# Delta-rule attention and a low-rank mixer on one core: k, q and z of every second head moved to the other half of the partitions

## The chip, the core and the metric

One core of one Trainium2 chip (trn2) runs the whole program in one launch. The metric is the device time of that core in microseconds (us). TensorE (PE, with its weight loads PEld) multiplies matrices, VectorE (DVE), ScalarE (ACT) and GpSimd (POOL) work on tiles in on-chip memory, and SyncE (SP) issues most of the loads and stores (DMA). A tile has 128 partitions; here nearly everything is cut in two halves of 64 partitions, `half(0)` and `half(1)`. Results of matmuls land in PSUM, from where ACT or DVE copies them.

## What is computed

The input has 4 batches, 8 heads, 768 tokens and a head width of 48. For each head a state matrix is updated token by token, and its output is the query times the state before the update:

```python
k_n = k / (np.linalg.norm(k, axis=-1, keepdims=True) + 1e-06)
for t in range(S):
    kt, vt, bt = (k_n[:, :, t], v[:, :, t], beta[:, :, t, None])
    y[:, :, t] = np.einsum('bhd,bhde->bhe', q[:, :, t], state)
    v_old = np.einsum('bhde,bhd->bhe', state, kt)
    state = state + bt[:, :, :, None] * np.einsum('bhd,bhe->bhde', kt, vt - v_old)
```

The heads' outputs are put side by side as x (4 x 768 x 384). The mixer follows, with rank 32 over the tokens and a hidden width of 1536 over the channels:

```python
xt = x.transpose(0, 2, 1)
h = xt @ U @ V
u = x + h.transpose(0, 2, 1)
ch = np.maximum(u @ w_ch1, 0.0) @ w_ch2
return (u + ch).astype(np.float32)
```

All is fp32.

## The kernel before

The kernel works on the recurrence in chunks of 64 tokens (`L`), 12 per batch (`NC`). Half a batch, six chunks (`UC`), is a unit; units 0 and 1 are batch 0, units 2 to 7 are batches 1 to 3. Within a chunk, the tokens' mutual effect is a triangular matrix that is inverted (blocks of 32, `BK`), so that a chunk needs a few matmuls only.

Eight heads are laid out as two groups `g` of four slots `s = 2*j + par`. Group g has its tokens on partitions `half(g)`. After a transpose, the head's channels are on `half(par)`. `QUADS` lists the four (par, g):

```python
QUADS = ((0, 0), (1, 1), (1, 0), (0, 1))
heads = [(j, par, g) for j in range(2) for par, g in QUADS]
def half(i, size=L):
    return slice(L * i, L * i + size)
```

The rows that a matmul reads and the partitions that it writes decide which part of the 128 x 128 array it uses: reading `half(a)` and writing `half(b)` uses one 64 x 64 quarter.

The load puts all four slots of a group on its half:

```python
for s in range(4):
    engines[queue].dma_start(
        out=t[L * g : L * g + L, :, s],
        in_=src[b, 4 * g + s, hf * UC * L : (hf + 1) * UC * L, :].rearrange("(c t) d -> t c d", t=L),
    )
```

The Gram products of keys with keys and queries, in `grams`, two chunks a group (L501):

```python
for par, g in QUADS:
    rows, cols = slice(DP * par, DP * par + D), slice(L * g, L * g + L)
    nc.tensor.matmul(p_g[cols, par, c, parts, j], kq[rows, c0 + c, j, 0, cols],
                     kq[rows, c0 + c, j, parts, cols], start=True, stop=True)
```

For units 2 to 7 `parts` covers keys and queries at once, so the moving operand is 128 wide; units 0 and 1 do them apart, 64 wide.

The blocks below the diagonal of the inverse, for units 2 to 7 (`split == 1`), are two chains of 32 x 32 matmuls, 24 (`CS`) for each g. p_x (L673) reads the partitions from L*g + 32 and writes from 32*g; p_v (L690) reads from 32*g and writes from L*g:

```python
for i in range(4):
    nc.sync.dma_start(out=diagonal(zt, i), in_=blk[i])
for g in range(2):
    nc.sync.dma_start(out=zc[BK * g : BK * g + BK], in_=blk[2 * g])
turned(zn, zc)
...
p_x = ps_pair("p_x")
nc.tensor.matmul(p_x[BK * g : BK * g + BK, x, at], pg[rows, c, r, j, 0:BK], zt[rows, c, r, j, BK:L], ...)
nc.scalar.copy(xz, p_x[0 : 2 * BK, :, 0 : CS // 2 * BK])
p_v = ps_pair("p_v")
nc.tensor.matmul(p_v[L * g : L * g + BK, x, at], zn[BK * g : BK * g + BK, e], xz[BK * g : BK * g + BK, x, at], ...)
```

One step of the recurrence, in `recur` (cut): `from_state` (L849) reads the old state, z is the inverse times the right-hand side (p_c, L886, batches 1 to 3 only), p_s (L901) is the state's update and L909 adds z's part to the output:

```python
def from_state(p, kq, cu, i, s_old, first):
    for j, par, g in heads:
        nc.tensor.matmul(p[half(g), par, ...], kq[half(par, D), cu, j, i, half(g)], s_old[half(par, D), g, j], ...)
...
p_c = ps_one([128, 4, D], "p_c")
for j, par, g in heads:
    nc.tensor.matmul(p_c[half(g), 2 * j + par], zt[half(g), cu, par, j], rhs[half(g), 2 * j + par], ...)
nc.scalar.copy(z, p_c)
...
p_s = ps_pair("p_s")
for j, par, g in heads:
    nc.tensor.matmul(p_s[half(par), g, D * j : D * j + D], kn[half(g), cu, 2 * j + par], z[half(g), 2 * j + par], ...)
for j, par, g in heads:
    nc.tensor.matmul(p_y[half(g), par, D * (2 + j) : D * (2 + j) + D], qk[half(g), cu, par, j], z[half(g), 2 * j + par], ...)
```

PSUM comes in three pools of two buffers each: "pair" (two banks, `ps_pair`), "one" and "mix" (one bank each).

The order of all instructions is made while the program is built: each part of the work is a generator that yields steps with estimated durations per engine (`step(pe=..., act=..., take=("pair",))`), and a loop places the step that could start first. In the early phase it also fills TensorE's idle time with matmuls of no use (`keep_busy`, L106). The channel mixing of one batch (p_f at L1006, p_o at L1026, six records a group) runs between the attention steps of the next.

Of the kernel before, what the change touches and what calls it, by code (L numbers as in the profile page):

```python
# [16 lines left out]
L = 64  # L17
BK = 32
# [7 lines left out]
def kernel(  # L26
# [9 lines left out]
    moe_w_ch2: bass.AP,  # L36
    out: bass.AP,
):

# [104 lines left out]
    def run():  # L146
# [61 lines left out]
        out=upper, in_=upper, pattern=[[1, 128]], base=0,  # L208
        channel_multiplier=-1, compare_op=ALU.is_gt, fill=0.0,
    )  # L210
    mask_u = const.tile([128, L], FP32, name="mask_u")
    for g in range(2):
        at = slice(L * g, L * g + L)
# [36 lines left out]
    def load_beta():  # L250
        yield step(then=3.5)
        yield step(pe=1.2, then=0.1, take=("one",))
        p_bt = ps_one([128, NB, B, H], "p_bt")
        for c in range(NB):
            nc.tensor.matmul(
                p_bt[:, c].rearrange("p b h -> p (b h)"),
                beta_sb[:, c * 128 : c * 128 + 128],
                ident[0 : B * H, 0 : B * H],
                start=True,
                stop=True,  # L260
            )
        yield step(dve=0.8, give=("one",))
        for g in range(2):
            for i in range(2):
                nc.vector.tensor_copy(
                    out=betas[L * g : L * g + L, i::2].rearrange("p c (b s) -> p c b s", b=B),
                    in_=p_bt[L * i : L * i + L, :, :, 4 * g : 4 * g + 4],
                )
        emitted(("betas", 0))
# [97 lines left out]
    def load(n):  # L367
# [7 lines left out]
        vn = raw[n] = unit.tile([128, UC, 4, D], FP32, name="vn")  # L375

        def tensor(name, t, src, queues):
            if queues[0] != queues[1]:
                yield step(**{names[x]: 2.6 for x in queues})
            for g in range(2):  # L380
                queue = queues[g]
                if queues[0] == queues[1]:
                    yield step(**{names[queue]: 2.6})
                for s in range(4):
                    engines[queue].dma_start(  # L385
                        out=t[L * g : L * g + L, :, s],
                        in_=src[b, 4 * g + s, hf * UC * L : (hf + 1) * UC * L, :].rearrange(
                            "(c t) d -> t c d", t=L
                        ),
                    )  # L390
            emitted((name, n), 4.1 if n == 0 else 5.0)
# [19 lines left out]
    def norms(n):  # L411
# [15 lines left out]
        norm = small.tile([128, UC, 4], FP32, name="norm")  # L427
        nc.vector.tensor_reduce(out=norm, in_=ksq, axis=AX.X, op=ALU.add)
        emitted(("ksq", n))
        yield step(act=0.25, then=0.1)  # L430
        nc.scalar.sqrt(norm, norm)
        yield need(("betas", 0))
        yield step(dve=0.95, then=0.1)
        nc.vector.tensor_scalar_add(norm, norm, 1e-6)
# [36 lines left out]
    def grams(n):  # L471
# [22 lines left out]
        def products(c0, parts):  # L494
            yield step(pe=0.8 if parts.stop - parts.start == 1 else 1.4, then=0.1, take=("pair",))
            p_g = ps_pair("p_g").rearrange("p r (c i j t) -> p r c i j t", c=2, i=2, j=2)
            for c in range(2):
                for j in range(2):
                    for par, g in QUADS:
                        rows, cols = slice(DP * par, DP * par + D), slice(L * g, L * g + L)  # L500
                        nc.tensor.matmul(  # L501
                            p_g[cols, par, c, parts, j],
                            kq[rows, c0 + c, j, 0, cols],
                            kq[rows, c0 + c, j, parts, cols],
                            start=True,
                            stop=True,
                        )
            keys, queries = parts.start == 0, parts.stop == 2
            yield step(
                act=0.6 if keys and n > 0 else 0,  # L510
# [53 lines left out]
    def blocks(n):  # L564
# [86 lines left out]

        blk = [scr2[CS * i : CS * i + CS].rearrange("q s t -> s q t") for i in range(4)]
        if split == 1:
            yield step(sp=3.6, then=2.2)
            zc = single.tile([2 * BK, CS, BK], FP32, name="zc", tag="zc")
            zn = single.tile([2 * BK, CS, BK], FP32, name="zn", tag="zn")
            for i in range(4):
                nc.sync.dma_start(out=diagonal(zt, i), in_=blk[i])
            for g in range(2):
                nc.sync.dma_start(out=zc[BK * g : BK * g + BK], in_=blk[2 * g])  # L660

            yield step(dve=1.0, then=-0.8)
            turned(zn, zc)
            for e in range(CS):
                if e % 8 == 0:
                    yield step(pe=0.57, take=("pair",) if e == 0 else ())
                if e == 0:
                    p_x = ps_pair("p_x")
                c, r, j = e // 4, e // 2 % 2, e % 2
                x, at = e // (CS // 2), slice(BK * (e % (CS // 2)), BK * (e % (CS // 2)) + BK)  # L670
                for g in range(2):
                    rows = slice(L * g + BK, L * g + L)
                    nc.tensor.matmul(  # L673
                        p_x[BK * g : BK * g + BK, x, at],
                        pg[rows, c, r, j, 0:BK],
                        zt[rows, c, r, j, BK:L],
                        start=True,
                        stop=True,
                    )
            yield step(act=0.8, then=0.1, give=("pair",))  # L680
            xz = single.tile([2 * BK, 2, CS // 2 * BK], FP32, name="xz", tag="zc")
            nc.scalar.copy(xz, p_x[0 : 2 * BK, :, 0 : CS // 2 * BK])
            for e in range(CS):
                if e % 8 == 0:
                    yield step(pe=0.57, take=("pair",) if e == 0 else ())
                if e == 0:
                    p_v = ps_pair("p_v")
                x, at = e // (CS // 2), slice(BK * (e % (CS // 2)), BK * (e % (CS // 2)) + BK)
                for g in range(2):
                    nc.tensor.matmul(  # L690
                        p_v[L * g : L * g + BK, x, at],
                        zn[BK * g : BK * g + BK, e],
                        xz[BK * g : BK * g + BK, x, at],
                        start=True,
                        stop=True,
                    )
            yield step(act=1.6, give=("pair",))
            for g in range(2):
                rows = slice(L * g, L * g + BK)
                nc.scalar.mul(  # L700
                    zt[rows].rearrange("p (x c) r j t -> p x (c r j) t", x=2)[:, :, :, BK:L],
                    p_v[rows, :, 0 : CS // 2 * BK].rearrange("p x (q t) -> p x q t", t=BK),
                    -1.0,
                )
            for third in range(3):
                emitted(("below", n, third), 0.2)
            return
# [137 lines left out]
    def recur(b):  # L845
        def from_state(p, kq, cu, i, s_old, first):

            for j, par, g in heads:
                nc.tensor.matmul(  # L849
                    p[half(g), par, D * (2 * i + j) : D * (2 * i + j) + D],  # L850
                    kq[half(par, D), cu, j, i, half(g)],
                    s_old[half(par, D), g, j],
                    start=first and j == 0,
                    stop=(i == 0),
                    skip_group_check=True,
                )
# [4 lines left out]
        for c in range(NC):  # L861
# [12 lines left out]
            if c > 0:  # L874
                for i in (0, 1) if b > 0 else (1, 0):
# [3 lines left out]
                nc.vector.tensor_tensor(  # L879
                    out=by_slot(rhs), in0=by_slot(raw[n][:, cu]), in1=pair_of(p_y), op=ALU.subtract  # L880
                )
            if b > 0:
                yield step(pe=0.4, then=0.1, take=("one",))
                p_c = ps_one([128, 4, D], "p_c")
                for j, par, g in heads:
                    nc.tensor.matmul(  # L886
                        p_c[half(g), 2 * j + par],
                        zt[half(g), cu, par, j],
                        rhs[half(g), 2 * j + par],
                        start=True,  # L890
                        stop=True,
                    )
                z = steps.tile([128, 4, D], FP32, name="z")
                yield step(act=0.33, then=0.1, give=("one",))
                nc.scalar.copy(z, p_c)  # L895

            yield step(pe=0.65, then=-0.2, take=("pair",) if c < NC - 1 else ())
            if c < NC - 1:
                p_s = ps_pair("p_s")
                for j, par, g in heads:  # L900
                    nc.tensor.matmul(  # L901
                        p_s[half(par), g, D * j : D * j + D],
                        kn[half(g), cu, 2 * j + par],
                        z[half(g), 2 * j + par],
                        start=True,
                        stop=True,
                    )
            for j, par, g in heads:
                nc.tensor.matmul(  # L909
                    p_y[half(g), par, D * (2 + j) : D * (2 + j) + D],  # L910
                    qk[half(g), cu, par, j],
                    z[half(g), 2 * j + par],
                    start=(c == 0 and j == 0),
                    stop=(j == 1),
                    skip_group_check=True,
                )
            yield step(
                dve=0.37 if c < NC - 1 else 0, act=0.65, on="dve", then=0.1,
                give=("pair", "pair") if c < NC - 1 else ("pair",),
            )  # L920
            if c < NC - 1:
                s_new = steps.tile([128, 2, 2, D], FP32, name="s")
# [168 lines left out]
```

## Time and profile before

| what | value |
|---|---|
| time, median of 3 runs | 717.27 us (716.61 to 717.34) |
| span in the profile | 715.6 us |
| PE busy | 669.1 us (93%) |
| PEld busy | 426.4 us (60%) |
| DVE busy | 325.6 us (45%) |
| ACT busy | 203.4 us (28%) |
| POOL busy | 42.5 us (6%) |
| p_f and p_o, PE busy | 201.0 and 201.2 us |

Busy time of PE counts the stretches in which at least one matmul is under way. Matmuls overlap, so a group's busy time is less than its count times the mean of one. A fp32 matmul shows as two records. In the lines of groups, `64*64 64x48` stands for the 64 rows and 64 columns of the array that the weights take, and for the moving operand, here 64 partitions by 48 elements; the number behind `x` is the count of records. Window and timeline views give times from the start of the span.

### The profile page before, as it was taken

The numbers are of one execution on the slowest core, as the hardware profiler recorded it, in microseconds if no ns is written. First come the engines' busy times: TensorE is split into PE (matmuls) and PEld (weight loads), VectorE is DVE, ScalarE is ACT, GpSimd is POOL, SyncE is SP. The second block draws the span as 40 slices with busy tenths as digits, with TensorE's granted clock in tenths as the row PEclk, the third lists the DMA queues.
The fourth block names the chain that finished last, engine by engine and source line by source line (L and its number), as shares of the span: only waits on it lengthen the run. The fifth ranks groups of instructions, "written<-read, shape, count | busy, mean of one in ns | idle before, by whom it ended". The sixth has DMA issues, their size and how long they took to land.

```text
span 715.6 us, 18968 instructions
## 1 busy us (share of the span) xinstructions
PE 669.1 (93%) x8370; PEld 426.4 (60%) x8370; DVE 325.6 (45%) x800; ACT 203.4 (28%) x468; POOL 42.5 (6%) x79
## 2 busy tenths in 40 slices
PE   6549999889999999889999999999999999899997
PEld 5336776646656566756566666556666665455554
DVE  7655777781775811459484113287483011200000
ACT  3314445454203211533122332243112311220110
POOL 4740010100000000000000000000000000000000
PEclk9768999999999999999999999999999999999999
DMA  8971558333124033351502050431402000000000
GB/s 142 210 155 33 128 122 203 104 67 74 40 55 79 4 66 64 66 115 31 111 13 63 12 97 25 92 66 30 84 23 57 3 12 24 1 0 23 11 1 33
DMA packets 140498, 45.37 MB, mean 63 GB/s; under 512 B 133568, under 2 KB 136640, under 8 KB 140416
## 3 DMA queue, kind: packets, MB, share of 16 engines
q1 hardware_dynamic: 130560, 30.39, 21.1%
q0 software_dynamic: 3552, 12.88, 6.4%
q10 hardware_dynamic: 6304, 0.89, 0.9%
q8 instruction: 66, 1.08, 0.7%
q14 instruction: 16, 0.13, 0.1%
HBM read 33.03 MB, written 11.11 MB: 62 GB/s over the span
## 4 chain that ended last, share of the span: by engine, by line
PE 82%; DVE 8%; DMA 4%; ACT 2%; SPq 2%; issue 1%; ACTq 0%; DVEq 0%
PE p_f L1006 27%; PE p_o L1026 24%; PE p_y L849 3%; PE p_c L886 3%; PE p_y L909 3%; PE p_g L501 3%; PE p_h L965 2%; PE p_s L901 2%; PE p_t L486 2%; DVE prod L621 2%; DVE xt L627 2%; SPq L385 2%; PE p_x L673 1%; PE p_v L690 1%; DVE x L969 1%
## 5 line engine op out<-in xcount | busy, mean ns | idle before, releaser
L1006 PE MATMUL p_f<-ut,w_sb 128*128 128x384 f32 x576 | 201.0, 494 | 1.1 <-ACT ut L976 1.1
L1026 PE MATMUL p_o<-w_sb,h_f 128*128 128x384 f32 x576 | 201.2, 495 | 0.6 <-DVE x L996 0.6
L1026 PEld LDWEIGHTS p_o<-w_sb,h_f 128*128 128x128 f32 x576 | 104.7, 190 | 65.2 <-DVE x L996 1.2
L1006 PEld LDWEIGHTS p_f<-ut,w_sb 128*128 128x128 f32 x576 | 104.4, 190 | 64.4 <-ACT ut L976 1.6
L991 ACT ACTIVATE h_f<-p_f 128x384 f32<-128x384 f32 x96 | 47.2, 491 | 185.9 <-PE p_f L1006 185.9
L996 DVE TENSOR_TENSOR x<-x,p_o 128x384 f32<-128x384 f32 x24 | 13.2, 553 | 134.8 <-PE p_o L1026 134.8
L627 DVE TENSOR_TENSOR xt<-xt,prod 96x112 f32<-96x112 f32 (+21 forms) x216 | 70.4, 326 | 7.4
L621 DVE TENSOR_TENSOR prod<-gs,xt 96x112 f32<-96x112 f32 (+21 forms) x216 | 70.0, 324 | 8.0 <-ACT xt L597 1.5
L924 DVE TENSOR_TENSOR s<-s,p_s 128x192 f32<-128x192 f32 x40 | 14.1, 354 | 77.1 <-PE p_s L901 77.0
L931 ACT COPY x<-p_y 64x192 f32<-64x192 f32 x96 | 30.1, 313 | 67.0 <-PE p_y L909 57.9
L879 DVE TENSOR_TENSOR rhs<-vn,p_y 128x192 f32<-128x192 f32 x44 | 15.5, 353 | 54.9 <-PE p_y L849 54.3
L492 ACT COPY kq<-p_t 128x512 f32<-128x512 f32 x48 | 27.9, 585 | 33.9 <-PE p_t L486 26.7
L849 PEld LDWEIGHTS p_y<-s,kq 48*64 48x64 f32 x1408 | 25.0, 134 | 18.8 <-issue 16.3
L895 ACT COPY z<-p_c 128x192 f32<-128x192 f32 x36 | 11.5, 320 | 70.2 <-PE p_c L886 69.5
L849 PE MATMUL p_y<-s,kq 48*64 48x48 f32 x1408 | 30.4, 222 | 0.2
L501 PEld LDWEIGHTS p_g<-kq 48*64 48x64 f32 x960 | 22.7, 137 | 12.8 <-issue 7.4
L501 PE MATMUL p_g<-kq 48*64 48x128 f32 (+1 forms) x960 | 28.6, 258 | 1.3 <-ACT kq L492 1.2
L577 POOL MEMSET xt<- 96x1056 f32 x6 | 5.9, 978 | 351.3 <-DMA scr<-xt 351.3
L886 PEld LDWEIGHTS p_c<-rhs,zt 64*64 64x64 f32 x528 | 18.6, 134 | 13.5 <-issue 7.9
L523 DVE TENSOR_TENSOR qk<-p_g,mask_u 128x256 f32<-128x256 f32 x48 | 18.0, 416 | 19.0 <-ACT pg L517 18.4
L886 PE MATMUL p_c<-rhs,zt 64*64 64x48 f32 x528 | 22.4, 222 | 2.1 <-DVE rhs L879 1.2
L909 PE MATMUL p_y<-z,qk 64*64 64x48 f32 x576 | 22.9, 218 | 0.9 <-ACT z L895 0.9
(149 smaller groups left out, 637.5 us busy)
## 6 DMA issues: line engine op xcount, KB each, us to landing
wide<-in_moe_w_ch_dram POOLq DMA_DIRECT2D x6, 768.0 KB, 5.4
stage<-in_moe_w_ch_dram POOLq DMA_DIRECT2D x6, 768.0 KB, 5.3
out_dram<-x SPq DMA_DIRECT2D x24, 192.0 KB, 1.9
kn<-in_k_dram SPq DMA_DIRECT2D x60, 72.0 KB, 4.0
qn<-in_q_dram SPq DMA_DIRECT2D x48, 72.0 KB, 2.4
vn<-in_v_dram SPq DMA_DIRECT2D x48, 72.0 KB, 2.4
gs<-scr SPq DMA_DIRECT2D x8, 384.0 KB, 3.7
scr<-xt SPq DMA_DIRECT2D x8, 384.0 KB, 3.0
```

Source lines behind the costliest of these rows:

```text
L492: nc.scalar.copy(places, p_t)
L501: nc.tensor.matmul(p_g[cols, par, c, parts, j], kq[rows, c0 + c, j, 0, cols], kq[rows, c0 + c, j, parts, cols], start=True, stop=True,)
L523: nc.vector.tensor_tensor(out=qk[:, at, par], in0=p_g[:, par, :, 1], in1=mask_u[:, None, None, :].to_broadcast([128, 2, 2, L]), op=ALU.mult,)
L621: nc.vector.tensor_tensor(out=prod, in0=gb[:, :, j : j + 1, j + 1 :].to_broadcast([NP, split, m, w]), in1=xb[:, :, 0:m, j : j + 1].to_broa ...
L627: nc.vector.tensor_tensor(out=xb[:, :, 0:m, j + 1 :], in0=xb[:, :, 0:m, j + 1 :], in1=prod, op=ALU.subtract,)
L849: nc.tensor.matmul(p[half(g), par, D * (2 * i + j) : D * (2 * i + j) + D], kq[half(par, D), cu, j, i, half(g)], s_old[half(par, D), g, j], ...
L886: nc.tensor.matmul(p_c[half(g), 2 * j + par], zt[half(g), cu, par, j], rhs[half(g), 2 * j + par], start=True, stop=True,)
L909: nc.tensor.matmul(p_y[half(g), par, D * (2 + j) : D * (2 + j) + D], qk[half(g), cu, par, j], z[half(g), 2 * j + par], start=(c == 0 and j ...
L931: nc.scalar.copy(tokens_of(b, c, g), pair_of(p_y, 1)[half(g)])
L991: nc.scalar.activation(hs[f], p_f, ACTF.Relu)
L1006: nc.tensor.matmul(p_f, w1_sb[:, t, f * 128 : (f + 1) * 128], ut[:, t], start=(t == 0), stop=(t == KT - 1),)
L1026: nc.tensor.matmul(p_os[c], hs[e][:, c * 128 : c * 128 + 128], w2_sb[:, e], start=(e == 0), stop=(e == FT - 1),)
```

## The change

Slots with odd `par` of k and q, and the right-hand side and z that go with them, are put on the other half of the partitions, so that the matmuls that read and write the same half use all four quarters of the array. v follows only in batch 0, where it is loaded crossed; in later batches p_c itself carries the odd heads across. The index `x` is now the half, not the head group. Where both are still mixed up, the kernel compensates: beta is transposed with a permuted identity (`swap`), the norms of odd heads are swapped by two small matmuls (`p_n2`), and the Gram products of odd heads write keys and queries to different halves, which needs two matmuls for each. p_c moves from a tile of its own to the spare part of the p_s tile. The blocks below the diagonal are spread over four tiles in each of the two chains. The diff, cut to its core (the rest renames g to x):

```diff
+    swap = const.tile([B * H, B * H], FP32, name="swap")
+    nc.gpsimd.tensor_copy(out=swap, in_=ident[0 : B * H, 0 : B * H])
+    for i in (0, 4):
+        nc.gpsimd.tensor_copy(
+            out=swap[:, i + 1 : i + 4 : 2], in_=ident[0 : B * H, 5 - i : 8 - i : 2]
+        )
...
-                ident[0 : B * H, 0 : B * H],
+                swap,
...
+            crossed = b == 0 or name != "v"
...
-                        out=t[L * g : L * g + L, :, s],
+                        out=t[half(g ^ (s % 2) if crossed else g), :, s],
...
-        yield step(act=0.25, then=0.1)
-        nc.scalar.sqrt(norm, norm)
+        if b == 0:
+            yield step(act=0.25, then=0.1)
+            nc.scalar.sqrt(norm, norm)
+        else:
+            yield step(pe=0.3, then=0.1, take=("one",))
+            p_n2 = ps_one([128, UC, 2], "p_n2")
+            for g in range(2):
+                nc.tensor.matmul(
+                    p_n2[half(g)], ident[:, half(1 - g)], norm[:, :, 1::2], start=True, stop=True
+                )
+            yield step(act=0.5, then=0.1, give=("one",))
+            nc.scalar.sqrt(norm[:, :, 0::2], norm[:, :, 0::2])
+            nc.scalar.sqrt(norm[:, :, 1::2], p_n2)
...
-                        nc.tensor.matmul(
-                            p_g[cols, par, c, parts, j],
+                        crossed = n > 1 and par == 1
+                        for i in (slice(0, 1), slice(1, 2)) if crossed else (parts,):
+                            to = half(1 - x) if crossed and i.start == 0 else cols
+                            nc.tensor.matmul(
+                                p_g[to, par, c, i, j],
...
-            zc = single.tile([2 * BK, CS, BK], FP32, name="zc", tag="zc")
+            HQ = CS // 2
+            zc = single.tile([128, HQ, BK], FP32, name="zc", tag="zc")
...
-            for g in range(2):
-                nc.sync.dma_start(out=zc[BK * g : BK * g + BK], in_=blk[2 * g])
+            for i in range(4):
+                x, g = divmod(i, 2)
+                nc.sync.dma_start(
+                    out=zc[BK * i : BK * i + BK], in_=blk[2 * g][:, HQ * x : HQ * x + HQ]
+                )
...
+            where = [(e, x, g) for e in range(HQ) for x in range(2) for g in range(2)]
+            yield step(pe=0.95, then=0.1, take=("one",))
+            p_x = ps_one([128, HQ, BK], "p_x")
+            for e, x, g in where:
+                q, rows, to = HQ * x + e, slice(L * g + BK, L * g + L), BK * (2 * x + g)
+                c, r, j = q // 4, q // 2 % 2, q % 2
+                nc.tensor.matmul(p_x[to : to + BK, e], pg[rows, c, r, j, 0:BK], zt[rows, c, r, j, BK:L], ...)
...
+            for e, x, g in where:
+                rows = slice(BK * (2 * x + g), BK * (2 * x + g) + BK)
+                nc.tensor.matmul(p_v[L * g : L * g + BK, x, BK * e : BK * e + BK], zn[rows, e], xz[rows, e], ...)
...
-                    p[half(g), par, D * (2 * i + j) : D * (2 * i + j) + D],
+                to = half(x if b == 0 and i == 0 else x ^ par)
+                    p[to, par, D * (2 * i + j) : D * (2 * i + j) + D],
...
-                yield step(pe=0.4, then=0.1, take=("one",))
-                p_c = ps_one([128, 4, D], "p_c")
+                yield step(pe=0.4, then=0.1, take=("pair",))
+                p_s = ps_pair("p_s")
-                        p_c[half(g), 2 * j + par],
-                        zt[half(g), cu, par, j],
-                        rhs[half(g), 2 * j + par],
+                        p_s[half(x), par, D * (2 + j) : D * (2 + j) + D],
+                        zt[half(x ^ par), cu, par, j],
+                        rhs[half(x ^ par), 2 * j + par],
-                nc.scalar.copy(z, p_c)
+                nc.scalar.copy(by_slot(z), pair_of(p_s, 1))
...
-                    p_y[half(g), par, D * (2 + j) : D * (2 + j) + D],
-                    qk[half(g), cu, par, j],
-                    z[half(g), 2 * j + par],
+                    p_y[half(x ^ par), par, D * (2 + j) : D * (2 + j) + D],
+                    qk[half(x), cu, par, j],
+                    z[half(x), 2 * j + par],
```

## The prediction, made blind

> **What bounds the kernel now.** I read the page first: the slices tell when TensorE is full, the chain of waits tells whose time it is.
>
> ```profile
> PE   6549999889999999889999999999999999899997
> PE 82%; DVE 8%; DMA 4%; ACT 2%; SPq 2%; issue 1%; ACTq 0%; DVEq 0%
> ```
>
> TensorE (PE) is 90% busy or more in most slices after the third, and 82% of the chain that ends last is its own work. A busy engine is not yet the bound, so I cut the span into stages (columns: window, busy time and count of each engine, PE clock, DMA share, GB/s):
>
> ```profile
> 150.00:606.00 456.00, 446.29 (x5554) 280.40 (x5554) 213.25 (x559) 128.61 (x287) 4.87 (x5) 1.00 0.24 51
> 606.00:623.00 17.00, 14.23 (x80) 7.61 (x76) 3.89 (x7) 4.18 (x10) 0.00 (x0) 1.00 0.00 1
> 623.00:716.00 93.00, 88.95 (x276) 52.06 (x274) 3.33 (x6) 11.32 (x24) 0.00 (x0) 1.00 0.04 13
> ```
>
> From 150 to 606 us the attention of batches 1 to 3 runs between the channel-mixing matmuls of the batch before. PE is busy 446 of 456 us (98%) at full clock, while VectorE (DVE) is at 213 of 456 (47%). A PE microsecond saved there should come off the span. From 623 us on only channel mixing is left, which the change does not touch. Before 150 us the kernel is a chain of loads, block inversion and weight conversion, with filler matmuls on PE.
>
> Now the cost of the matmuls that the change touches (columns: line, engine, form, count | busy us, mean ns of one | idle before):
>
> ```profile
> L909 PE MATMUL p_y<-z,qk 64*64 64x48 f32 x576 | 22.9, 218 | 0.9 <-ACT z L895 0.9
> L886 PE MATMUL p_c<-rhs,zt 64*64 64x48 f32 x528 | 22.4, 222 | 2.1 <-DVE rhs L879 1.2 <-issue 0.9
> L501 PE MATMUL p_g<-kq 48*64 48x128 f32 x576 | 19.8, 275 | 0.6 <-ACT kq L492 0.6
> ...
> L901 PE MATMUL p_s<-z,kn 64*64 64x48 f32 x528 | 14.8, 227 | 1.0 <-DVE qk L523 0.6 <-ACT z L895 0.5
> ...
> L673 PE MATMUL p_x<-zt,pg 32*32 32x32 f32 x576 | 10.6, 192 | 0.0
> L690 PE MATMUL p_v<-xz,zn 32*32 32x32 f32 x576 | 10.6, 192 | 0.0
> ...
> L501 PE MATMUL p_g<-kq 48*64 48x64 f32 x384 | 8.9, 234 | 0.7 <-ACT kq L492 0.6
> ```
>
> An fp32 matmul leaves two records: 36 steps (c of batches 1 to 3) x 8 matmuls are 288, and p_c has 528 + 48 = 576. The telling pair is p_c and p_s: same shape, same number, 22.4 us against 14.8. In the timeline (start, duration, what, count):
>
> ```profile
> 237.13 0.67 PE L886 MATMUL p_c<-rhs,zt 64*64 64x48 f32 x16
> 237.72 2.20 PE L1006 MATMUL p_f<-ut,w_sb 128*128 128x384 f32 x6
> 239.86 0.45 PE L901 MATMUL p_s<-z,kn 64*64 64x48 f32 x16
> 240.12 0.63 PE L909 MATMUL p_y<-z,qk 64*64 64x48 f32 x16
> 240.69 0.59 PE L1006 MATMUL p_f<-ut,w_sb 128*128 128x384 f32 x1
> ```
>
> From its first start to the next group's, p_s takes 0.26 us, p_y 0.57, p_c 0.59. Taking the last one's duration off the group (0.67 - 0.22, 0.45 - 0.23, 0.63 - 0.22) and dividing by 15 intervals, records start 30, 15 and 27 ns apart. The code says why: p_s reads rows of half g and writes half par, so its four (par, g) pairs are four quarters of the array; p_c and p_y at L909 read half g and write half g, so they use two of the four. Per quarter that is one record in about 60 ns in all three.
>
> **What the Trainium skill says.** "TensorEngine Tiling (Array Packing)", section "Tiling Modes", says that tiles work independently and can load weights and multiply in parallel, with four of them at 64x64. The trace agrees: twice the quarters, half the interval. The same page, "Gotcha 1: PSUM Pressure", says that different row tiles cannot access one PSUM bank at the same time. Here p_c writes a single bank from both row halves, to different partition halves, and its pace per quarter is that of p_s, which gives each row half a bank of its own; so no such cost is seen, and I expect none from the new placing, where both row halves share a bank on disjoint partitions. "TensorE: Matmul & The Clock Gate", section "Back-to-back issue gap", lists an issue floor of about 25 ns for small matmuls; p_s records start 15 ns apart over four quarters, so the measurement decides, and what the floor is for eight or more a wave no run here shows yet.
>
> **The change part by part.**
>
> *z on four quarters (p_c).* Odd heads of k, q (and z) now lie on the other half, so p_c reads half x^par and writes half x. 16 records at 15 instead of 30 ns: 0.225 us less per step (0.448 - 0.223). 36 steps: **-8.1 us**.
>
> *Output product on four quarters (p_y, L909).* Reads half x, writes half x^par: the same 0.2 to 0.24 us, 36 steps: **-8.1 us**. Batch 0 has 12 such groups as well, but before 150 us; see below.
>
> *Blocks below the diagonal (p_x, p_v).* Each uses two 32x32 tiles now and four after (eight different ones over both). 96 records a group at (1.77 - 0.19) / 95 = 16.6 ns, where 1.77 = 10.6 / 6 units. Half of that is 48 x 16.6 = 0.8 us a group, 12 groups: **-9.5 us** if four tiles really run at 8 ns a record. That is a faster stream of starts than anything in this trace sustains (the best is 15), so I count three quarters: **-7 us**.
>
> *Gram products (p_g).* For units 2 to 7 the odd heads' keys and queries now go to different halves, so each of their 128-wide products becomes two 64-wide ones: 32 records a group become 16 of 128 and 32 of 64. A quarter takes 4 x (1.10 - 0.275) / 31 = 106 ns for a 128-wide record, and 4 x (0.74 - 0.234) / 31 = 65 ns for a 64-wide one (1.10 = 19.8 / 18 groups, 0.74 = 8.9 / 12). The lower two quarters then have 16 x 65 = 1.04 us where they had 8 x 106 = 0.85: 0.19 us more, 18 groups: **+3.4 us**.
>
> *Norms.* Units 2 to 7 get two small matmuls (p_n2) that swap the halves of the odd heads' norms, and a second square root. A visit of PE costs its start as well as its records; from the p_ct rows and the 0.1 us that each group's first records take longer, I take 0.25 us a visit, 6 visits: **+1.5 us**. The extra ACT operation (about 0.22 us, the duration of the square root at L431) is on an engine at 28%.
>
> *Off the path.* The DVE transpose zn goes from 64x768 (967 ns) to 128x384, some 0.56 us by the 426 ns of its 128x256 form; the ACT copy xz from 792 to about 0.48 us. zc is loaded by four DMAs in place of two, same bytes. DVE and ACT have room, so I count nothing.
>
> *The start.* Three POOL copies build the swapped identity before the p_bt matmuls, which sit on the first stretch: POOL copies there take 0.24 us each, so up to +0.7 us. Batch 0's twelve output products save 12 x 0.22 = 2.7 us of PE; from 60 to 126 us the chain is on PE with its fillers, but from 127 to 158 us it is on DVE converting weights, which will take most of that back. Together **-0.5 us**.
>
> Sum: -8.1 - 8.1 - 7 + 3.4 + 1.5 - 0.5 = -18.8 us. The schedule is made at build time from estimated durations and now shifts; PE idles 2% in the stage already, and a shorter visit may meet a DVE or ACT result a little sooner than it is ready. A tenth off, -17 to -19: I take 717.3 - 18.3 = **699.0 us**.
>
> **The rivals.**
>
> *The recurrence's latency takes over.* Per step p_y, rhs (DVE 0.35), p_c, z (ACT 0.32), p_s, s (DVE 0.35) form a chain. Bare it is about 3 us, and one step takes 8.4 us in the trace (p_c at 228.69 and 237.13), because a 2.13 us group of p_f stands in every gap. There is slack, so I give this one chance in ten; the time would be about 708.
>
> *A new wait for PSUM.* p_c now lives in the two-buffer "pair" pool, in the tile that p_s uses later. So from p_c to the state update both pairs are taken, and the p_g and p_v groups have to find their place elsewhere. For it: 2.7 us of each step's 8.4. Against it: PE can run p_f meanwhile. If the groups pile up at a batch's end, as PE's idle from 606 to 623 us suggests is possible, it gives back 3 to 8 us: 703 to 708.
>
> *Small tiles bound by issue, not by the array.* If 16 records of 32x32 cannot start faster than now, p_x and p_v give nothing: 699 + 7 = 706.
>
> *Everything pays in full.* p_x and p_v at half, p_g nearly free because the quarters overlap: 693.
>
> **Range and chances.** The 2% line is 702.9 us. The first two parts (16 us) rest on a measured pair of rows and alone reach 701, but the added p_g and p_n2 work takes 5 back; p_x and p_v decide on which side it falls. Range 691 to 707; faster 0.72, within 2% 0.26, slower 0.02.
>
> **What would show each step.** p_c busy near 0.45 us a group (16 us in all) and p_y at L909 the same; p_x and p_v near 1.0 us a group; p_g at 1.2 to 1.3 us; PE busy down by some 20 us, with the stage of 446 us ending about 18 us sooner and the last 93 us unchanged. The prediction is wrong if p_x stays near 1.7 us, if p_g grows by much more than 0.2 us, if the idle share of PE in the middle stage rises above 4%, or if the first 150 us move by more than 2 us.

## The result and the profile after

The changed kernel takes 710.37 us (median of 4 runs, 708.26 to 711.82) against 717.31 us before: a ratio of 0.990, 95% interval 0.986 to 0.993. It is 6.9 us faster where 18.3 were forecast. That is within 2%, for which the prediction gave a chance of 0.26, and the time lies above its range of 691 to 707.

The groups that were to get cheaper did so. These rows of the changed kernel (line, engine, form, count | busy us, mean ns of one | idle before) stand against those of before; p_c is now the `p_s<-rhs,zt` row:

```profile
L939 PE MATMUL p_y<-z,qk 64*64 64x48 f32 x576 | 15.7, 226 | 1.0 <-ACT z L924 1.0
L915 PE MATMUL p_s<-rhs,zt 64*64 64x48 f32 x528 | 15.5, 234 | 4.7 <-DVE qk L549 3.0 <-DVE rhs L906 1.7
...
L981 PE MATMUL p_tt<-x,u_sb 128*32 128x384 f32 x48 | 9.8, 759 | 0.3 <-ACT kq L514 0.3
...
L715 PE MATMUL p_v<-xz,zn 32*32 32x32 f32 x576 | 6.6, 194 | 0.0
...
L701 PE MATMUL p_x<-zt,pg 32*32 32x32 f32 x576 | 6.1, 193 | 0.0
```

p_y at L939 went from 22.9 to 15.7 us, p_c from 24.4 to 16.8 (with its 48 records of vn, the values that the first step takes as they are), p_x from 10.6 to 6.1, p_v from 10.6 to 6.6: 23.3 us. p_g, all forms together, went from 28.6 to 33.3 and p_n2 is new with 1.9. The sum is -16.7 us, but PE's busy time fell by 8.2 only (669.1 to 660.9). Something made other matmuls dearer: p_tt, which the change does not touch, went from 6.2 to 9.8 us, p_h from 19.4 to 21.4. Its row before:

```profile
L951 PE MATMUL p_tt<-x,u_sb 128*32 128x384 f32 x48 | 6.2, 495 | 0.0
```

And p_c has a new wait, on the masked product qk, which DVE makes of p_g.

The clock row of the page before, and two rows of the changed kernel's page, tell where:

```profile
PEclk9768999999999999999999999999999999999999
...
PE   7639999899999999879999999999999998999998
...
PEclk9867999999999999779999999999999998899999
```

Before, the row has 9 in every slice after the fourth. Now it dips around 290 us and again near 600. By stretches (window, busy time and count of PE, PEld, DVE, ACT and POOL, then the granted PE clock, DMA share and GB/s):

```profile
139.93:143.35 3.42, 1.81 (x53) 1.30 (x52) 3.38 (x5) 1.00 (x4) 1.28 (x2) 1.00 0.46 105
290.13:293.54 3.41, 2.01 (x73) 1.56 (x64) 2.12 (x3) 1.49 (x3) 0.00 (x0) 1.00 0.29 54
293.54:310.61 17.07, 12.83 (x267) 9.25 (x257) 3.17 (x9) 4.27 (x11) 0.00 (x0) 0.50 0.22 39
593.91:597.32 3.41, 1.81 (x80) 1.47 (x80) 0.85 (x3) 0.95 (x3) 0.00 (x0) 1.00 0.16 58
597.32:607.56 10.24, 9.03 (x56) 4.55 (x56) 1.67 (x3) 1.89 (x5) 0.00 (x0) 0.50 0.01 2
```

For 17.1 us and again for 10.2 us PE ran at half its clock, each time after 3.4 us in which it was busy only 53 to 59%. (A third, 3.4 us long, follows the first window, at 143.35 us.) Both stretches begin in the tail of a recurrence, when the channel mixing of the batch before is used up and nothing fills PE between the steps. Batch 1's tail, in the timeline of PE (start, duration, what, count, idle before and who ended it), first from the kernel before, then from the changed one:

```profile
284.14 2.20 PE L1026 MATMUL p_o<-w_sb,h_f 128*128 128x384 f32 x6
...
307.19 1.64 PE L951 MATMUL p_tt<-x,u_sb 128*32 128x384 f32 x12
```

```profile
279.15 2.20 PE L1056 MATMUL p_o<-w_sb,h_f 128*128 128x384 f32 x6
...
292.11 0.45 PE L915 MATMUL p_s<-rhs,zt 64*64 64x48 f32 x16 [0.97 <-DVE qk L549]
...
295.33 2.01 PE L527 MATMUL p_g<-kq 48*64 48x128 f32 x48
...
298.89 0.68 PE L915 MATMUL p_s<-rhs,zt 64*64 64x48 f32 x16 [0.52 <-DVE qk L549]
...
302.16 2.01 PE L527 MATMUL p_g<-kq 48*64 48x128 f32 x48
...
305.73 0.68 PE L915 MATMUL p_s<-rhs,zt 64*64 64x48 f32 x16 [1.56 <-DVE qk L549]
...
307.53 2.77 PE L981 MATMUL p_tt<-x,u_sb 128*32 128x384 f32 x12
```

Two things stand there. p_c does not read qk; by the code it waits because p_g holds a "pair" buffer until DVE has made qk of it, and p_y holds the other. And the group of p_g takes 2.01 us at half clock, where it takes 1.17 at full clock later in the trace. At p_o's last group the changed kernel is 5.0 us ahead (279.15 against 284.14 us). From there to p_tt it takes 28.4 us, against 23.1 before, so that p_tt of batch 1 starts at 307.5 us, against 307.2: the whole lead is lost in the tail.

Stage lengths in us, cut at the starts of p_tt in each timeline, with the experiments described below. The tail, from the start of p_o's last group to p_tt, is a part of batch 1:

| kernel | start | batch 1 | its tail | batch 2 | batch 3 | rest |
|---|---|---|---|---|---|---|
| before | 143.6 | 163.6 | 23.1 | 151.5 | 148.6 | 108.3 |
| changed | 144.0 | 163.5 | 28.4 | 147.7 | 143.9 | 111.0 |
| e1, p_c in p_y's tile | 143.5 | 161.3 | 24.7 | 142.9 | 143.7 | 110.4 |
| e2, fillers in the tails | 142.4 | 161.4 | 26.6 | 146.3 | 144.0 | 107.9 |
| e3, both | 140.6 | 158.4 | 22.4 | 143.7 | 144.0 | 108.0 |

### The profile page after: what moved, and what is told of

The parts are those of the page before. It is cut to its first block, busy times and chain, and to the rows that moved or that the text cites. A ratio compares the mean times of both kernels' runs of the same rounds, so it can differ in the third digit from the quotient of the medians.

```text
span 710.1 us, 19662 instructions
## 1 busy us (share of the span) xinstructions
PE 660.9 (93%) x8682; PEld 411.6 (58%) x8682; DVE 323.5 (46%) x800; ACT 201.6 (28%) x474; POOL 42.7 (6%) x82
## 4 chain that ended last, share of the span: by engine, by line
PE 54%; DVE 1%; issue 1%; DMA 1%; ACT 0%; SPq 0%; DVEq 0%; ACTq 0%
PE p_o L1056 21%; PE p_f L1036 20%; PE p_h L995 2%; PE p_y L876 2%; PE p_g L527 2%; PE p_s L915 2%; PE p_s L931 1%; PE p_t L508 1%; PE p_tt L981 1%; PE p_y L939 1%; PE p_u L1003 1%; DVE x L999 1%; PE p_v L715 1%; DMA gs<-scr 1%; PE p_x L701 1%
## 5 line engine op out<-in xcount | busy, mean ns | idle before, releaser
L527 PEld LDWEIGHTS p_g<-kq 48*64 48x64 f32 x1248 | 28.2, 149 | 13.9 <-issue 8.2
L527 PE MATMUL p_g<-kq 48*64 48x64 f32 (+1 forms) x1248 | 33.3, 253 | 1.9 <-ACT kq L514 1.9
L924 ACT COPY z<-p_s 128x192 f32<-128x192 f32 x36 | 11.5, 319 | 64.9 <-PE p_s L915 64.9
L995 PE MATMUL p_h<-tt,v_sb 128*128 128x384 f32 x48 | 21.4, 554 | 2.4 <-DVE tt L987 2.1
L915 PEld LDWEIGHTS p_s<-rhs,zt 64*64 64x64 f32 x528 | 11.5, 140 | 19.3 <-issue 11.6
L999 DVE TENSOR_TENSOR x<-x,p_h 128x384 f32<-128x384 f32 x24 | 13.3, 554 | 20.3 <-PE p_h L995 19.7
```

Source lines behind the costliest of these rows:

```text
L527: nc.tensor.matmul(p_g[to, par, c, i, j], kq[rows, c0 + c, j, 0, cols], kq[rows, c0 + c, j, i, cols], start=True, stop=True,)
L915: nc.tensor.matmul(p_s[half(x), par, D * (2 + j) : D * (2 + j) + D], zt[half(x ^ par), cu, par, j], rhs[half(x ^ par), 2 * j + par], start ...
L995: nc.tensor.matmul(p_h, v_sb[:, c * 128 : (c + 1) * 128], tt, start=True, stop=True)
L999: nc.vector.tensor_tensor(out=x[:, c], in0=x[:, c], in1=p_h, op=ALU.add)
```

## Experiments

Two theories for the missing 11 us: **C**, the halved clock, which a shorter PE visit (the time that PE works between two waits) may bring on because the waits around it stay as long as they were; **P**, the wait for a pair buffer that p_c now has to hold. Each ratio is to the kernel before on the same chip, where its median was 719.0 to 719.7 us; microseconds given back against the changed kernel are differences of these ratios times 717.

**e1, p_c in the p_y tile.** It takes columns of that tile which nobody uses, so the second pair is taken at p_s again:

```diff
-            taken = c < NC - 1 or b > 0
+            taken = c < NC - 1
...
-                yield step(pe=0.4, then=0.1, take=("pair",))
-                p_s = ps_pair("p_s")
+                yield step(pe=0.4, then=0.1)
...
-                        p_s[half(x), par, D * (2 + j) : D * (2 + j) + D],
+                        p_y[half(x), par, D * (4 + j) : D * (4 + j) + D],
...
-                        start=True,
+                        start=(c == 0 and j == 0),
...
-                nc.scalar.copy(by_slot(z), pair_of(p_s, 1))
+                nc.scalar.copy(by_slot(z), pair_of(p_y, 2))
...
-            yield step(pe=0.65, then=-0.2, take=("pair",) if taken and b == 0 else ())
+            yield step(pe=0.65, then=-0.2, take=("pair",) if taken else ())
...
+                p_s = ps_pair("p_s")
```

> The changed kernel with p_c moved into spare columns of the p_y tile, so that the second pair buffer is taken at p_s again, not at p_c. Theory P (the shortfall is the new wait for a pair buffer): the three waits of p_c on the masked product qk (0.97, 0.52 and 1.56 us near 292 to 305 us) go, the tail of batch 1's recurrence shrinks from 26 to some 22 us, PE stays busy enough to keep its clock there, and the time is 702 to 705 us. Theory C (the shortfall is the halved PE clock, which comes from any idle in a tail): the waits on qk go, but the half-clock stretch near 597 us stays, and if that near 294 us stays too the time is 707 to 709 us.

Measured: 702.51 us, ratio 0.977 (0.973 to 0.980). p_c's waits on qk are gone (p_s has one of 0.75 us), and 9.3 us (0.013 x 717) come back. The time is in P's range, but P's step that PE would keep its clock failed: in this trace it ran at half for 13.7 us from 294.6 us on and for 6.8 from 591.6 on. So neither theory is right alone. PE's timeline of e1 in the same tail:

```profile
294.72 1.10 PE L876 MATMUL p_y<-s,kq 48*64 48x48 f32 x32 [3.02 <-DVE s L953]
295.58 2.04 PE L527 MATMUL p_g<-kq 48*64 48x128 f32 x48
```

Here the state's sum s on DVE came 3 us late. The build-time order also moved with this edit, so its 9.3 us are the wait and the order together; only 3.0 us of waits on qk are seen as such, all in batch 1's tail. The table says the same: batch 1 gives 2.2 us of the gain, and batch 2, where the changed kernel has no wait on qk, gives 4.8, with 141.1 us of PE work in place of 145.6. Most of what e1 gave back is thus not shown to be the wait.

**e2, fillers in the tails.** The changed kernel with a 128x256 matmul of no use, whose result nobody reads, where PE waits for DVE and for ACT:

```diff
+    def stir():
+        t = psum.tile([128, 512], FP32, name="stir", tag="mix", bufs=2)
+        nc.tensor.matmul(t[:, 0:256], ident, idle_sb, start=True, stop=True)
...
+            tail = (b == 1 and c >= 7) or (b == 3 and c >= 10)
...
+                if tail:
+                    stir()
...
+                if tail:
+                    stir()
```

The first `stir()` stands ahead of p_c, the second ahead of p_s. The build's clock does not know of them, so the order of all other instructions stays exactly as it was.

> The changed kernel with one matmul of no use (128x256, result unread) ahead of p_c and of p_s in the last five steps of batch 1's recurrence and the last two of batch 3's, where PE waits about 0.5 us for DVE and ACT. Theory C: the PE clock stays at full through both tails, p_tt falls back from 2.8 to 1.5 us, p_g there from 2.0 to 1.2 us, and about 9 us come back: 700 to 703 us. Theory P: the waits on qk remain, the fillers only add up to 14 x 0.4 us of PE, and the time stays at 709 to 713 us.

Measured: 705.72 us, ratio 0.981 (0.978 to 0.985): some 6 us back, where C expected 9 and P none; the time lies between the two ranges. The clock row of its page:

```profile
PEclk9868999999999999999999999999999999999999
```

And two rows of its PE timeline in batch 1's tail:

```profile
300.75 0.70 PE L112 MATMUL stir<-w_sb,ident 128*128 128x256 f32 x2
302.37 0.45 PE L922 MATMUL p_s<-rhs,zt 64*64 64x48 f32 x16 [0.93 <-DVE qk L553]
```

With more matmuls the kernel got faster, and the wait on qk is still there: the half clock is a loss of its own, apart from P. The last stage is back at 107.9 us, below the 108.3 of before. The short stretch near 143 us is missing from this trace too, though no filler stands there, so what this trace gains ahead of batch 1's tail is not the fillers' work.

**e3, both edits.**

> Both edits together: p_c in the p_y tile and the matmuls of no use in the tails. Theory C: full clock as with the fillers alone, and the waits on qk gone as well: 697 to 701 us. Theory P: no better than with p_c in the p_y tile alone, 702 to 706 us.

Measured: 697.96 us, ratio 0.970 (0.967 to 0.973). The two effects nearly add up: 0.013 and 0.008 apart, 0.020 together. This is the fastest version of all, and it stands where the forecast had put the changed kernel.

**e4, the old blocks below the diagonal** in the changed kernel (p_x, p_v, zc, zn and xz as before).

> The changed kernel with the old blocks below the diagonal: p_x and p_v on two tiles each, 96 records at 16.6 ns. By the sum of the parts it gives back the 8.5 us that the groups' busy times fell by: 717 to 720 us. If the clock is what counts, the longer p_x and p_v lie far from the tails and change nothing there, so the whole 8.5 us should appear; if less than 4 us appear, the parts' savings are lost in the schedule.

Measured: 719.81 us (20 runs), ratio 1.001 (0.999 to 1.003), 8 us above the changed kernel. So within the changed kernel the blocks gave their 8.5 us, and k, q and z on the other half gave nothing net: what they saved went into p_g, p_n2, p_c's new place and the clock, as e1, e2 and e7 bear out. The runs of this kernel spread from 715.0 us at a mean granted clock of 0.968 to 723.4 at 0.950, the same program each time.

**e5, only the blocks**, put into the kernel before.

> The kernel before with only the blocks below the diagonal spread over four tiles a chain; k, q and z stay where they were. By the sum of the parts p_x and p_v fall from 21.2 to some 12.7 us and nothing else moves: about 8.5 us less, ratio to before near 0.988. If undoing this part in the changed kernel cost 8 us only because of where its clock drops happened to fall, this run gives less than half of that, ratio above 0.994.

Measured: 713.41 us, ratio 0.991 (0.988 to 0.995): about 6 us, somewhat under the expected 8.5. Its p_x and p_v are at 6.1 us each, and its trace has three half-clock stretches of 3.4 us that the kernel before does not have, at 150, 552 and 604 us. That these account for the rest is not shown.

**e6, the control**: the fillers of e2 in the kernel before.

> Control: the kernel before, which keeps its full clock from 59 us on, with the same matmuls of no use in the same steps. Theory C (the fillers help only by keeping the clock): no gain, ratio to before 0.999 to 1.004. If the fillers help in some other way (a different order of the steps, for one), the ratio is below 0.996 here too.

Measured: 721.85 us, ratio 1.0036 (1.0016 to 1.0055). Where no long stretch at half clock is to be avoided, fourteen fillers cost 2.6 us. Their gain in e2 is the clock.

**e7, k, q and z without the side effects**: the old blocks, p_c in the p_y tile, and the fillers.

> The changed kernel without the spread blocks, but with p_c in the p_y tile and the fillers in the tails: k, q and z on the other half alone, freed of both the pair wait and the half clock. If the two side effects are what ate this part (it was worth nothing in the changed kernel), it is now worth p_c 7.6 + p_y 7.2 less p_g 2 to 3 and p_n2 1.9, some 10 to 11 us: ratio to before 0.984 to 0.987. If its gain is lost elsewhere in the schedule, the ratio stays above 0.993.

Measured: 704.73 us, ratio 0.981 (0.979 to 0.984), 13.6 us, even more than the parts' sum. This part of the change was worth nothing in the changed kernel; with p_c out of the second pair buffer and the tails filled it is worth the larger share of e3's gain. The fillers alone gain nothing in the kernel before (e6), but p_c in spare columns of the p_y tile was not tried there, so a share of the 13.6 us may belong to that.

**e8, e3 with fewer fillers** (batch 1 from c = 9 on, in place of 7).

> p_c in the p_y tile, and the matmuls of no use in the last three steps of batch 1's recurrence and the last two of batch 3's, ten in place of fourteen. If the clock needs a window of some 3.4 us with PE busy under about 60% to drop, and no such window opens in the first two tail steps, the clock still holds and the four fillers' time (up to 0.6 us each) is saved: ratio to before 0.967 to 0.970. If a window opens there, the half clock comes back near 285 to 290 us and the ratio is 0.974 or more.

Measured: 701.98 us, ratio 0.977 (0.974 to 0.981), the second case. Not in the first two tail steps, though: a window opened right between the fillers. PE is the first busy time of the row, 1.54 of 3.41 us:

```profile
291.86:295.27 3.41, 1.54 (x79) 1.34 (x80) 1.63 (x3) 1.21 (x3) 0.00 (x0) 1.00 0.02 4
```

That was the busy time of the window; this is the timeline in it:

```profile
292.75 1.36 DVE L492 TENSOR_TENSOR vn<-vn,norm 128x1152 f32<-128x1152 f32 x1 [1.37 <-DMA scrc<-cts]
294.03 0.35 DVE L962 TENSOR_TENSOR s<-s,p_s 128x192 f32<-128x192 f32 x1
294.52 0.68 PE L880 MATMUL p_y<-s,kq 48*64 48x48 f32 x32 [1.87 <-DVE s L962]
```

DVE runs in order; the scaling of vn for the next unit stands ahead of s and waits for a transfer, so PE sits for 1.87 us, is busy 45% of the window, and the clock halves for 6.8 us at 295.3 us. In e3 the same p_y waits 0.31 us. In e1 the same scaling waited 2.07 us for that transfer, ahead of the 3.02 us wait shown there. How many fillers are enough therefore seems to depend on when that transfer lands.

**e9, the fillers in batch 3's tail alone.**

> The changed kernel with the four matmuls of no use in the last two steps of batch 3's recurrence alone. Theory C for each tail by itself: only the half-clock stretch near 597 us goes, the last stage from p_tt to the end falls from 111.0 to 108 us, the stretch near 294 us stays, and the ratio to before is 0.985 to 0.987, against 0.990 for the change itself and 0.981 with both tails filled. If the ratio is 0.982 or less, the fillers of batch 1 were not needed; if it is 0.989 or more, the last tail's clock costs nothing.

Measured: 707.06 us, ratio 0.984 (0.981 to 0.987). The stretch near 600 us is gone, the last stage takes 108.0 us, and the one from 291.8 us stays for 17.1 us. The last stage gives 3.0 us (111.0 to 108.0); in time it is 4.1 us (0.990 to 0.984) of e2's 6, just over what was expected.

## Why the prediction was wrong, point by point

- *p_c and p_y on four quarters*: right. Forecast -8.1 us each, measured -7.6 and -7.2 in busy time, part of them at half clock; in e2, at full clock, p_y is at 15.0 and p_c at 14.8 + 1.3, which is -7.9 and -8.3 (with p_c's 48 records of vn).
- *p_x and p_v*: the full -9.5 us would have been nearer than the -7 that I counted; -8.5 in busy time, 8 us in the run that took them away again, 6 in the one that had them alone. A group takes 1.02 us (6.1 / 6), a record every 8.7 ns. The rival of a bound by issue is refuted.
- *p_g*: right. At full clock a group takes 1.10 us from its start to the next one's (438.32 to 439.42 us), before 0.89 (437.51 to 438.40): +0.21 us, forecast 0.19. *Norms*: 0.22 us a visit from p_n2's start to the next group's (286.11 to 286.33 us), forecast 0.25.
- *The start*: -0.5 forecast, +0.4 measured (143.6 to 144.0). Small, and the traces in the table differ by up to 3.4 us there.
- *The PSUM rival* was right in its mechanism: p_c waits 3.0 us for a pair buffer. Its size is not settled, for e1's 9.3 us hold the order's share too; and 3 to 8 us on 699 make 702 to 707, not 703 to 708. It stood as a rival and not in the sum. I had its 2.7 us a step before me and argued that PE can run p_f meanwhile. In the tails there is no p_f.
- *The step that failed* is the sentence "a PE microsecond saved there should come off the span". For idle time I spoke of a tenth off, which would have been 1.9 us, and took off 0.5. In place of that step the runs show two losses in the tails and around them: the half clock, some 6 us (e2, with e6 as its control), and p_c's hold on a second pair buffer with the order that came of it, 9.3 us (e1). With both removed 14 us come back (0.990 to 0.970).
- *The clock* of 1.00 in the stage's row was taken as given. The lower clock comes with k, q and z on the other half, with the pair wait or without it: the mean granted clock of a run was 0.964 to 0.980 in 44 runs of the kernel before and 0.969 to 0.981 with the blocks alone (e5), but 0.956 to 0.961 in the changed kernel, 0.950 to 0.968 without its blocks (e4) and 0.956 to 0.965 in e1. The likely route is that the saving shortens PE's visits and leaves the waits between them as they are, so that PE's busy share in the tails falls. That is argued, not shown. The tail before had it close already: from 604.0 to 607.4 us PE is busy 2.37 of 3.40 us (70%), and there the clock held; e5, with the p_c and p_y of before, lost it at 603.56 us after the same share (2.38 of 3.41 us). My sign for it, an idle share above 4% in the middle stage, was the wrong view: over batches 1 to 3 it rose from 2.6 to 3.5% only, and the work itself got slower.

What stays open: how much of e1's gain is the wait and how much the new order, why e7 gives 3 us more than its parts, and what exactly makes the clock drop.

## What to carry to other kernels

Where matmuls get shorter in a latency-bound stretch the waits around them stay, and the clock may halve there and in what follows, as it did here for 17.1 and 10.2 us. Look at the granted clock row and at the stretch that is left without filling work, not at the average, and put work or fillers there. When an intermediate result moves into a buffer that is held longer, count who else needs that pool in the stretch where nothing else can run; spare columns of a tile that is held anyway were free here. And judge each part of a composite change by taking it away alone, then ask what holds back a part that gives nothing: here the blocks, forecast at 7 of 18.8 us, carried the whole gain, until the rest was freed.

## What the runs showed of the hardware

At 597 us the PE clock halved without PE standing still for long: in the 3.4 us ahead of the drop it was busy 1.81 us, and the waits in it were 0.57 us at most. It then stayed at half for 10.2 us though PE was busy 9.03 of them. "TensorE: Matmul & The Clock Gate" in the Trainium skill ties the drop to an idle window of about 3.4 us (section "What's actually happening"), and in "A second HAM failure mode: psum-queue depth-cycling" to short idles between groups, without a share. The drop at 597 us is of the second kind. Ahead of the drops PE was busy 53 and 59% in the changed kernel, 42% in e9 (1.42 of 3.40 us) and 70% in e5, while the changed kernel kept its clock in a window with 2.10 of 3.41 us busy:

```profile
607.56:610.97 3.41, 2.10 (x9) 1.02 (x8) 0.56 (x1) 0.49 (x2) 0.00 (x0) 1.00 0.00 0
```

The kernel before kept it even with 1.67 of 3.41 us busy (49%, from 143.96 to 147.37 us). So the traces give no busy share at which the clock drops. And four 32x32 tiles of the array take a record every 8.7 ns on average, well under the issue floor of about 25 ns that the prediction quoted from the same page.
